# Delta-rule attention and two expert layers: the last three row tiles become two, one of them 288 rows wide

## The chip, the cores and the metric

The kernel runs on one core of one Trainium2 chip. The metric is the device time of one execution in microseconds (us). Three timed runs of the kernel before took 984.87, 984.94 and 985.98 us; the median is 984.94. One further execution was profiled: its span, from the first to the last instruction, is 974.3 us.

## The reference

Three layers follow each other. First attention with a delta rule: for each of 4 x 8 heads a 48 x 48 state runs over 768 tokens.

```python
for t in range(S):
    kt, vt, bt = (k_n[:, :, t], v[:, :, t], beta[:, :, t, None])
    y[:, :, t] = np.einsum('bhd,bhde->bhe', q[:, :, t], state)
    v_old = np.einsum('bhde,bhd->bhe', state, kt)
    state = state + bt[:, :, :, None] * np.einsum('bhd,bhe->bhde', kt, vt - v_old)
```

The result is laid out as 3072 rows of 384. Each row then goes to one of 8 experts, by the largest of 8 logits, and is weighted by its softmax share.

```python
logits = x @ w_gate + modality_bias[modality_id]
e_idx = np.argmax(logits, axis=1)
...
    h = np.maximum(x[mask] @ w1[e], 0.0)          # 384 -> 1024
    out[mask] = gate_w[mask, None] * (h @ w2[e])  # 1024 -> 384
```

The third layer, here called the second expert, is the same for all rows: the largest of three products with 384 x 768 weights, then a product with 768 x 384.

```python
h = np.maximum(np.maximum(x @ w1, x @ w2), x @ w3)
return (h @ w_out).astype(np.float32)
```

## The kernel before, in words

Attention is done in 12 chunks of 64 tokens (C = 0 to 11). After each chunk its 256 rows are routed (route, L696): VectorE finds each row's expert and place, and POOL scatters the rows into xs, a table in DRAM with RS rows for each expert. Rows are then taken from xs in row tiles: a tile is up to 256 rows of one expert. select (L744) picks an expert on VectorE, in some ten operations on one partition, and writes the expert's number and the first row into ssel, which has one buffer; SP reads it into registers (L791, L792) and issues the tile's loads. A selection after chunks 1 to 10 wants an expert with a full 256 rows; the final ones take the expert with the most rows left. After the last chunk 256 zero rows are copied behind each expert's last row (pad_zero, L780: eight DMAs), so that a tile that is not full reads zero rows. Those have a row number past the end, and their output is dropped.

So there are 13 tiles: one after each of the chunks 1 to 11, then one more of 256 rows and one of 128. If rows are left after that, a loop on the device (L973) takes further tiles of 256; its count comes from remaining (L764).

Numbers are kept as two 16-bit parts, so each product is three matmuls. For a tile of w rows, tiles (L900) makes eight steps f:

- up (L819): the product hp of 128 hidden columns with the tile's rows mxT, 9 matmuls of w columns; ScalarE and VectorE split it into hh and hl.
- down (L835): 9 matmuls of w columns from hh and hl into accA (two products) and accB (one), which stand in PSUM over all eight steps.
- behind (L894): in steps 0 to 5 the tile before gets a step of the second expert (second, L856), 27 matmuls of its own width into pa (two products) and pb; ScalarE copies the first product to mt, VectorE takes the maximum with the other two, ScalarE and POOL split it into H. In steps 6 and 7 comes outp (L878): 18 matmuls of 384 columns for each 128 rows, scaled by ScalarE, scattered to the output by POOL.

After step 7, mid (L849) turns accA and accB into x2T, which the second expert reads. Weights come per step into ws (L802) through SP's DMA queue, with two buffers, and are split by ScalarE (wh) and POOL (wl).

The last tile's second expert runs alone, with nothing beside it (L925). PSUM has eight banks: two for accA and accB (psA), three in a ring (psM, tag m) which hp, pa, pb and po share, and three for attention (psC, psZ).

The order on each engine is made in two ways. The first part of the program is played as a list of steps in program order; from the bar in STEPS on, a scheduler orders the instructions of each engine by priorities, with a model of the engines. What side() wraps is placed ahead. The order is fixed when the program is built.

Of the kernel before, what the change touches and what calls it, by code (L numbers as in the profile page):

```python
# [7 lines left out]
F32 = mybir.dt.float32  # L8
# [11 lines left out]
RS = 3072 + 256  # L20
ZROW = 8 * RS
XROWS = ZROW + 256
XW = 784
# [94 lines left out]
class Kern:  # L118
# [29 lines left out]
    # ---------------------------------------------------------------- setup  # L148
    def setup(self):
# [24 lines left out]
        # room that the second expert's weights take later  # L174
# [7 lines left out]
    def zeros(self, eng, what, x, i=0):  # L182
        """A zeroed tile: only its diagonal blocks are written later."""
# [152 lines left out]
    # ---------------------------------------------------------------- keys and queries of a group  # L336
# [97 lines left out]
    # ---------------------------------------------------------------- key products and 32-token inverses  # L434
# [74 lines left out]
    # ---------------------------------------------------------------- preparation of a chunk  # L509
# [121 lines left out]
    # ---------------------------------------------------------------- chain  # L631
# [63 lines left out]
    # ---------------------------------------------------------------- routing  # L695
# [68 lines left out]
    def remaining(self):  # L764
# [5 lines left out]
        E.tensor_scalar(out=a, in0=a, scalar1=MAGIC, scalar2=MAGIC, op0=ALU.add, op1=ALU.subtract)  # L770
        r = mx.tile([1, 1], F32, name="sthr")
# [16 lines left out]
    # ---------------------------------------------------------------- experts  # L788
    def tile_load(self, si, w=256):
        nc, mx = self.nc, self.tp["x"]  # L790
        e = nc.sync.value_load(si[0:1, 0:1], min_val=0, max_val=7)  # L791
        row = nc.sync.value_load(si[0:1, 1:2], min_val=0, max_val=ZROW)  # L792
        T = dict(e=e, w=w, ws={}, wb={})
        T["xT"] = mx.tile([128, 6, 256], F16, name="mxT", bufs=3)[:, :, 0:w]
        nc.sync.dma_start_transpose(out=T["xT"], in_=self.xs[bass.ds(row, w), 0:384].bitcast(F16))
        T["ix"] = mx.tile([128, 2, 2], I32, name="ix", bufs=3)
        nc.sync.dma_start(out=T["ix"][:, 0:w // 128], in_=self.xs[bass.ds(row, w), 384:386].rearrange("(t p) w -> p t w", p=128))
# [4 lines left out]
    def wt_load(self, T, f):  # L802
        nc, e = self.nc, T["e"]
        ws = self.tp["w"].tile([128, 2, 384], F32, name="ws")
# [5 lines left out]
    def wt_cast(self, T, f):  # L810
        ws = T["ws"].pop(f)
        wh = self.tp["w"].tile([128, 2, 384], F16, name="wh", bufs=2)
        wl = self.tp["w"].tile([128, 2, 384], BF16, name="wl", bufs=2)
        with self.side():
            self.nc.scalar.activation(wh, ws, AF.Copy)  # L815
            self.lo("p", wl, ws, wh)
        T["wb"][f] = wh, wl

    def up(self, T, f):  # L819
        nc, mx, xT, w = self.nc, self.tp["x"], T["xT"], T["w"]  # L820
        wh, wl = T["wb"][f]
        h = self.tp["psM"].tile([128, 256], F32, name="hp", tag="m")[:, 0:w]
# [5 lines left out]
        hh = mx.tile([128, 256], F16, name="hh", bufs=2)[:, 0:w]  # L828
        hl = mx.tile([128, 256], F16, name="hl", bufs=2)[:, 0:w]
# [4 lines left out]

    def down(self, T, f):  # L835
        nc, w = self.nc, T["w"]
        if f == 0:
            pa = self.tp["psA"].tile([128, 2, 256], F32, name="accA")[:, :, 0:w]
            pb = self.tp["psA"].tile([128, 1, 256], F32, name="accB")[:, :, 0:w]
            T["acc"] = pa, pb  # L840
        hh, hl = T["h"]
        wh, wl = T["wb"].pop(f)
        pa, pb = T["acc"]
        for d, ps in enumerate((pa[:, 0], pa[:, 1], pb[:, 0])):
            ds = slice(128 * d, 128 * d + 128)
            for i, (a, b) in enumerate(((wh, hh), (wl, hh), (wh, hl))):
                nc.tensor.matmul(ps, lhsT=a[:, 1, ds], rhs=b, start=(f == 0 and i == 0 and d != 1), stop=(f == 7 and i == 2 and d > 0))  # L847

    def mid(self, T):  # L849
        x2T = T["x2T"] = self.tp["x"].tile([128, 6, 256], F16, name="x2T", tag="mxT", bufs=3)[:, :, 0:T["w"]]  # L850
        for ps, k, n in zip(T.pop("acc"), (0, 2), (2, 1)):
# [4 lines left out]
    def second(self, T, f):  # L856
        nc, mx, x2T, w = self.nc, self.tp["x"], T["x2T"], T["w"]
        if f == 0:
            T["H"] = {x: mx.tile([128, 6, 256], F16, name="H" + x, tag="H" + x) for x in "hl"}
# [10 lines left out]
        mt = mx.tile([128, 256], F32, name="mt", tag="ob", bufs=2)[:, 0:w]  # L870
        with self.side():
# [3 lines left out]
            nc.scalar.activation(T["H"]["h"][:, f, 0:w], mt, AF.Copy)  # L875
            self.lo("p", T["H"]["l"][:, f, 0:w], mt, T["H"]["h"][:, f, 0:w])

    def outp(self, T, t):  # L878
        nc, H = self.nc, T["H"]
        ts = slice(128 * t, 128 * t + 128)  # L880
        po = self.tp["psM"].tile([128, 384], F32, name="po", tag="m")
# [132 lines left out]
```

## Time and profile before

| | us |
|---|---|
| timed runs, median of 3 | 984.94 (984.87 to 985.98) |
| profiled execution, span | 974.3 |
| between the span and the median | 10.6 |
| eleventh tile's eight steps | 39.41 |
| twelfth tile's eight steps | 39.40 |
| thirteenth tile's eight steps (128 rows) | 33.39 |
| its second expert alone | 13.09 |
| from TensorE's last matmul to the end | 9.06 |

The page gives the profiled execution no total beside its span; 10.6 us is what lies between the span and the median of the timed runs. A window row gives a stretch, its length, and for each engine the busy time and the number of instructions; PEclk is the granted share of TensorE's full clock, 1.00 or 0.50. In a timeline a row's first number is the start, the second the duration; a matmul's duration overlaps the next one's, so the pitch is read from starts. What stands in brackets is the idle time of the engine just ahead and what ended it.

### The profile page before, as it was taken

The numbers are of one execution on the slowest core, as the hardware profiler recorded it, in microseconds if no ns is written. First come the engines' busy times: TensorE is split into PE (matmuls) and PEld (weight loads), VectorE is DVE, ScalarE is ACT, GpSimd is POOL, SyncE is SP. The second block draws the span as 40 slices with busy tenths as digits, with TensorE's granted clock in tenths as the row PEclk, the third lists the DMA queues.
The fourth block names the chain that finished last, engine by engine and source line by source line (L and its number), as shares of the span: only waits on it lengthen the run. The fifth ranks groups of instructions, "written<-read, shape, count | busy, mean of one in ns | idle before, by whom it ended". The sixth has DMA issues, their size and how long they took to land. (4 is left out here: it accounts for less than half of the span.)

```text
span 974.3 us, 25386 instructions
## 1 busy us (share of the span) xinstructions
PE 715.9 (73%) x9748; PEld 597.9 (61%) x9748; DVE 651.2 (67%) x1581; ACT 446.1 (46%) x894; POOL 553.7 (57%) x708
## 2 busy tenths in 40 slices
PE   1314610686359877678779877999899989999995
PEld 0213510575238666466568666788787868888885
DVE  7798897778896599859998589656464442222221
ACT  3436532674356453444446433364554534434432
POOL 7264366646767777446776478555546444444461
PEclk9999855697669999788899999999999999999998
DMA  7786688776796747665777743555532354423320
GB/s 114 175 167 166 107 216 207 186 146 159 195 222 133 179 115 176 135 140 131 161 170 192 147 110 92 125 144 99 141 85 91 106 192 122 115 82 107 97 68 19
DMA packets 360349, 134.76 MB, mean 138 GB/s; under 512 B 291225, under 2 KB 351655, under 8 KB 360096
## 3 DMA queue, kind: packets, MB, share of 16 engines
q1 hardware_dynamic: 357088, 123.56, 55.3%
q0 software_dynamic: 3136, 9.54, 2.7%
q8 instruction: 78, 1.28, 0.6%
q14 instruction: 47, 0.39, 0.1%
HBM read 80.45 MB, written 33.79 MB: 117 GB/s over the span
## 5 line engine op out<-in xcount | busy, mean ns | idle before, releaser
L138 POOL TENSOR_TENSOR wl<-ws,wh 128x768 bf16<-128x768 f32 x104 | 172.2, 1656 | 75.9 <-ACT wh L815 73.7
L868 PE MATMUL pa<-x2T,mwh 128*128 128x256 f16 (+1 forms) x936 | 170.6, 277 | 17.4 <-DVE x2T L140 10.2
L868 PEld LDWEIGHTS <-mwh 128*128 128x128 f16 x1404 | 137.4, 100 | 29.0 <-issue 11.7
L826 PE MATMUL hp<-mxT,wh 128*128 128x256 f16 (+1 forms) x624 | 125.0, 278 | 40.2 <-ACT wh L815 36.0
L868 PE MATMUL pa<-x2T,mwl 128*128 128x256 f16 (+1 forms) x468 | 128.0, 277 | 0.0
L138 POOL TENSOR_TENSOR Hl<-mt,Hh 128x256 f16<-128x256 f32 (+1 forms) x78 | 52.0, 666 | 116.1 <-ACT Hh L875 114.0
L815 ACT ACTIVATE wh<-ws 128x768 f16<-128x768 f32 x104 | 87.4, 840 | 38.8 <-PE accB L847 20.1
L832 DVE SCALAR_TENSOR_TENSOR hl<-hp,hh 128x256 f16<-128x256 f32 (+1 forms) x104 | 42.5, 409 | 77.7 <-ACT hh L831 77.0
L826 PEld LDWEIGHTS <-wh 128*128 128x128 f16 x624 | 62.0, 101 | 46.3 <-ACT wh L815 37.2
L868 PE MATMUL pb<-x2T,mwh 128*128 128x256 f16 (+1 forms) x468 | 89.6, 270 | 1.0 <-DVE mt L873 1.0
L144 PEld LDWEIGHTS <-bkh 128*128 128x128 f16 x560 | 55.2, 105 | 55.8 <-DVE bkh L432 23.9
L826 PE MATMUL hp<-mxT,wl 128*128 128x256 f16 (+1 forms) x312 | 86.1, 279 | 2.8 <-POOL wl L138 2.8
L502 DVE TENSOR_TENSOR stmp<-At,W 128x31 f32<-128x31 f32 (+29 forms) x155 | 83.2, 537 | 3.3 <-POOL At L491 0.3
L138 POOL TENSOR_TENSOR pl<-Pm,ph 64x512 f16<-64x512 f32 x48 | 56.9, 1185 | 50.2 <-ACT ph L628 41.3
L868 PEld LDWEIGHTS <-mwl 128*128 128x128 bf16 x702 | 69.9, 100 | 18.6 <-issue 10.2
L875 ACT ACTIVATE Hh<-mt 128x256 f16<-128x256 f32 (+1 forms) x78 | 31.7, 407 | 95.7 <-DVE mt L874 95.5
L847 PEld LDWEIGHTS <-wh 128*128 128x128 f16 x624 | 61.9, 101 | 20.0 <-issue 11.0
L504 DVE TENSOR_TENSOR W<-W,stmp 128x31 f32<-128x31 f32 (+29 forms) x155 | 71.3, 460 | 3.0
L873 DVE TENSOR_TENSOR mt<-pa,mt 128x256 f32<-128x256 f32 (+1 forms) x78 | 32.1, 411 | 59.7 <-ACT mt L872 55.1
L847 PE MATMUL accA<-hh,wh 128*128 128x256 f16 (+1 forms) x208 | 57.6, 277 | 9.5 <-ACT hh L831 9.2
L868 PE MATMUL pb<-x2T,mwl 128*128 128x256 f16 (+1 forms) x234 | 62.7, 270 | 0.0
L847 PE MATMUL accA<-hl,wh 128*128 128x256 f16 (+1 forms) x208 | 57.6, 279 | 5.5 <-DVE hl L832 5.3
(277 smaller groups left out, 2590.5 us busy)
## 6 DMA issues: line engine op xcount, KB each, us to landing
ws<-in_moe_w_dram SPq DMA_DIRECT2D x208, 192.0 KB
nd<-in_moe_w_dram SPq DMA_DIRECT2D x18, 384.0 KB
vf<-in_v_dram SPq DMA_DIRECT2D x48, 96.0 KB
ring<-in_k_dram SPq DMA_DIRECT2D x10, 384.0 KB
ring<-in_q_dram SPq DMA_DIRECT2D x10, 384.0 KB
xs<-xs SPq DMA_DIRECT2D x8, 392.0 KB
N<-Wd SPq DMA_DIRECT2D x48, 64.0 KB
Qdh<-tmh SPq DMA_DIRECT2D x6, 512.0 KB
```

The costliest lines, as they stand in the source:

```text
L138: nc.gpsimd.tensor_tensor(out=out, in0=in_, in1=hi, op=ALU.subtract)
L144: mm(out, lhsT=ah, rhs=bh, start=start, stop=False)
L502: E.tensor_tensor(out=tv, in0=At[:, j:j + 1, j + 1:].to_broadcast([128, m, n]), in1=W[:, r0:r1, j:j + 1].to_broadcast([128, m, n]), op=ALU ...
L504: E.tensor_tensor(out=W[:, r0:r1, j + 1:], in0=W[:, r0:r1, j + 1:], in1=tv, op=ALU.subtract)
L815: self.nc.scalar.activation(wh, ws, AF.Copy)
L826: nc.tensor.matmul(h, lhsT=a[:, 0, kk * 128:(kk + 1) * 128], rhs=xT[:, b], start=(n == 0), stop=(n == 8))
L832: nc.vector.scalar_tensor_tensor(out=hl, in0=h, scalar=0.0, in1=hh, op0=ALU.max, op1=ALU.subtract)
L847: nc.tensor.matmul(ps, lhsT=a[:, 1, ds], rhs=b, start=(f == 0 and i == 0 and d != 1), stop=(f == 7 and i == 2 and d > 0))
L868: nc.tensor.matmul(ps[i], lhsT=self.mw[a][:, i, kk, fs], rhs=x2T[:, b], start=(n == 0), stop=(n == 8))
L873: nc.vector.tensor_tensor(out=mt, in0=ps[1], in1=mt, op=ALU.max)
L875: nc.scalar.activation(T["H"]["h"][:, f, 0:w], mt, AF.Copy)
```

## The change

The tiles after chunks 1 to 10 stay. The selection after the last chunk and the two final ones become two final selections: the first for a tile of up to 288 rows, the second for one of 256. Attention's pools are closed ahead of them, and the wide tile gets pools of its own in the room that becomes free: its x tiles (mxw) and three accumulators of one bank each (psAw: accA, accC, accB). In the ring psM its second expert takes three buffers for each step, pa, pc and pb, one for each product, where a tile of 256 takes two. Each expert's room in xs, the zero rows and the pad copies grow from 256 to 288 rows; the zero rows are written by three DMAs. The wide tile's output has three pieces, of 128, 128 and 32 rows; the second and the third both come in step 7. Functions that had fixed widths take them from the tile.

```diff
-RS = 3072 + 256
+WIDE = 288
+RS = 3072 + WIDE
 ZROW = 8 * RS
-XROWS = ZROW + 256
+XROWS = ZROW + WIDE
...
+    def wide_pools(self, ctx):
+
+        return dict(self.tp, psA=self.pool(ctx, "psAw", 1, space=PSUM), x=self.pool(ctx, "mxw", 1), W=WIDE)
...
     def zero_rows(self):
-        self.nc.sync.dma_start(out=self.xs[ZROW:XROWS, :].rearrange("(r p) d -> p r d", p=128), in_=self.zero.to_broadcast([128, 2, XW // 2]))
+        for r, n in ((ZROW, 128), (ZROW + 128, 128), (ZROW + 256, WIDE - 256)):
+            self.nc.sync.dma_start(out=self.xs[r:r + n, :], in_=self.zero[0:n, 0])
...
         E.tensor_scalar(out=a, in0=a, scalar1=MAGIC, scalar2=MAGIC, op0=ALU.add, op1=ALU.subtract)
+        E.tensor_scalar_max(out=a, in0=a, scalar1=0.0)
...
     def pad_rows(self, r):
-        self.nc.sync.dma_start(out=self.xs[bass.ds(r, 256), :], in_=self.xs[ZROW:XROWS, :])
+        self.nc.sync.dma_start(out=self.xs[bass.ds(r, WIDE), :], in_=self.xs[ZROW:XROWS, :])
...
-        T["xT"] = mx.tile([128, 6, 256], F16, name="mxT", bufs=3)[:, :, 0:w]
+        T = dict(e=e, w=w, tp=tp, ws={}, wb={}, cols=[(t, min(128, w - t)) for t in range(0, w, 128)])
+        T["xT"] = mx.tile([128, 6, w], F16, name="mxT", bufs=3)
...
+        if w > 128 * full:
+            nc.sync.dma_start(out=T["ix"][0:w - 128 * full, full], in_=self.xs[bass.ds(row + 128 * full, w - 128 * full), 384:386])
...
+    def triple(self, pool, w, names, tag=None):
+
+        if w > 256:
+            ts = [pool.tile([128, w], F32, name=n, **(dict(tag=tag) if tag else {})) for n in names]
+            return ts, [(k, 1, t) for k, t in enumerate(ts)]
+        a = pool.tile([128, 2, w], F32, name=names[0], **(dict(tag=tag) if tag else {}))
+        b = pool.tile([128, w], F32, name=names[2], **(dict(tag=tag) if tag else {}))
+        return [a[:, 0], a[:, 1], b], [(0, 2, a), (2, 1, b)]
...
         if f == 0:
-            pa = self.tp["psA"].tile([128, 2, 256], F32, name="accA")[:, :, 0:w]
-            pb = self.tp["psA"].tile([128, 1, 256], F32, name="accB")[:, :, 0:w]
-            T["acc"] = pa, pb
+            T["acc"], T["out"] = self.triple(T["tp"]["psA"], w, ("accA", "accC", "accB"))
...
-        pa = self.tp["psM"].tile([128, 2, 256], F32, name="pa", tag="m")
-        pb = self.tp["psM"].tile([128, 256], F32, name="pb", tag="m")
-        ps = [pa[:, 0, 0:w], pa[:, 1, 0:w], pb[:, 0:w]]
+        ps, _ = self.triple(T["tp"]["psM"], w, ("pa", "pc", "pb"), "m")
...
         if f < 6:
             self.second(T, f)
-        elif f - 6 < T["w"] // 128:
-            self.outp(T, f - 6)
+        for t in range(len(T["cols"])):
+            if f == min(6 + t, 7):
+                self.outp(T, t)
...
-        if C >= 1:
-            self.sis.append((self.select(C == self.NC - 1),))
+        if 1 <= C < self.NC - 1:
+            self.sis.append((self.select(False),))
...
         self.play(then)
+        self.actx.close()
+        self.sis.append((self.select(True, WIDE), self.wide_pools(self.ctx)))
         self.sis.append((self.select(True),))
-        self.sis.append((self.select(True, 128), 128))
         for _ in self.moe:
             pass
-        self.actx.close()
         ri = self.remaining()
```

On VectorE after the last chunk, the first place shows the end of the selections, with the tile counter srem, and mid of the ninth tile (x2T). Before:

```order
L760 TENSOR_TENSOR ssel<-sred,zc 1x2
L770 TENSOR_SCALAR skey<-skey 1x8
L758 TENSOR_REDUCE sred<-sprod 1x2
L772 TENSOR_REDUCE sthr<-skey 1x1
L774 CAST srem<-sthr 1x1
L832 SCALAR_TENSOR_TENSOR hl<-hp,hh 128x256
L140 SCALAR_TENSOR_TENSOR x2T<-accA,x2T 128x512
L760 TENSOR_TENSOR ssel<-sred,zc 1x2
L140 SCALAR_TENSOR_TENSOR x2T<-accB,x2T 128x256
```

On VectorE at the same place after the change:

```order
L777 TENSOR_SCALAR skey<-skey 1x8
L779 TENSOR_REDUCE sthr<-skey 1x1
L781 CAST srem<-sthr 1x1
L844 SCALAR_TENSOR_TENSOR hl<-hp,hh 128x256
L766 TENSOR_TENSOR ssel<-sred,zc 1x2
L844 SCALAR_TENSOR_TENSOR hl<-hp,hh 128x256
L141 SCALAR_TENSOR_TENSOR x2T<-accA,x2T 128x512
L141 SCALAR_TENSOR_TENSOR x2T<-accB,x2T 128x256
```

Of the two writes of ssel shown before one is gone, and the other stands ahead of both pieces of x2T.

On SP after the pad copies, the second place shows the register loads (ssel, srem) and the eleventh tile's transposing load. Before:

```order
L791 TENSOR_LOAD ssel
L791 ISA x2
L792 TENSOR_LOAD ssel
L792 ISA x2
L972 TENSOR_LOAD srem
L972 ISA x2
L791 TENSOR_LOAD ssel
L791 ISA x2
L792 TENSOR_LOAD ssel
L792 ISA x2
L795 ISA
L795 DMA_TRANSPOSE mxT<-xs 128x6x256
```

On SP at the same place after the change:

```order
L800 TENSOR_LOAD ssel
L800 ISA x2
L801 TENSOR_LOAD ssel
L801 ISA x2
L993 TENSOR_LOAD srem
L993 ISA x2
L804 ISA
L804 DMA_TRANSPOSE mxT<-xs 128x6x288
```

One selection's register loads are gone; the load stands at the same place, 32 columns wider.

On VectorE in the closing stretch, the third place shows mid of the second tile from the end and the first step behind it (hl is the last tile's, mt the second expert's). Before:

```order
L140 SCALAR_TENSOR_TENSOR x2T<-accA,x2T 128x512
L140 SCALAR_TENSOR_TENSOR x2T<-accB,x2T 128x256
L832 SCALAR_TENSOR_TENSOR hl<-hp,hh 128x128
L873 TENSOR_TENSOR mt<-pa,mt 128x256
L874 TENSOR_TENSOR mt<-pb,mt 128x256
```

On VectorE at the same place after the change:

```order
L141 SCALAR_TENSOR_TENSOR x2T<-accA,x2T 128x288
L141 SCALAR_TENSOR_TENSOR x2T<-accC,x2T 128x288
L141 SCALAR_TENSOR_TENSOR x2T<-accB,x2T 128x288
L844 SCALAR_TENSOR_TENSOR hl<-hp,hh 128x256
L893 TENSOR_TENSOR mt<-pc,mt 128x288
L894 TENSOR_TENSOR mt<-pb,mt 128x288
```

The twelfth tile of 256 rows stood there with the 128-row tile behind it; now the wide tile stands there with the 256-row tile behind it, and each product has a buffer of its own.

## Rows read from the trace of the kernel before

**Rows 1.** the page: busy us (share of the span) xinstructions; then one costly group

```profile
PE 715.9 (73%) x9748; PEld 597.9 (61%) x9748; DVE 651.2 (67%) x1581; ACT 446.1 (46%) x894; POOL 553.7 (57%) x708
...
L815 ACT ACTIVATE wh<-ws 128x768 f16<-128x768 f32 x104 | 87.4, 840 | 38.8 <-PE accB L847 20.1
```

**Rows 2.** windows of closing stages: stretch, length; busy (x) per engine; PEclk, DMA

```profile
839.91:879.32 39.41, 39.41 (x345) 33.45 (x343) 9.52 (x22) 16.20 (x32) 19.07 (x16) 1.00 0.35 101
879.32:918.72 39.40, 39.40 (x343) 33.46 (x342) 9.52 (x22) 16.20 (x32) 19.06 (x16) 1.00 0.33 97
918.72:952.11 33.39, 33.13 (x353) 28.41 (x351) 8.46 (x22) 13.80 (x32) 17.43 (x15) 1.00 0.27 84
952.11:965.20 13.09, 12.41 (x180) 10.78 (x179) 4.05 (x14) 4.13 (x15) 3.53 (x7) 1.00 0.04 14
965.20:974.26 9.06, 0.00 (x0) 0.00 (x0) 0.00 (x0) 0.58 (x1) 0.99 (x1) 0.70 0.03 9
```

**Rows 3.** timeline of TensorE: start us, us, engine, line, operation, names, shape

```profile
845.96 0.27 PE L826 MATMUL hp<-mxT,wh 128*128 128x256 f16 x1
...
850.87 0.27 PE L826 MATMUL hp<-mxT,wh 128*128 128x256 f16 x1
...
957.59 0.22 PE L868 MATMUL pa<-x2T,mwh 128*128 128x128 f16 x1
...
962.11 0.33 PE L885 MATMUL po<-moh,Hh 128*128 128x384 f16 x1
...
964.87 0.33 PE L885 MATMUL po<-moh,Hl 128*128 128x384 f16 x1
```

**Rows 4.** timeline of TensorE around 800: in brackets idle time and releaser

```profile
801.04 0.38 PE L868 MATMUL pa<-x2T,mwh 128*128 128x256 f16 x2 [2.96 <-DVE x2T L140]
...
806.30 0.28 PE L826 MATMUL hp<-mxT,wh 128*128 128x256 f16 x1 [1.77 <-ACT wh L815]
```

**Rows 5.** timeline of VectorE around 800

```profile
800.50 0.15 DVE L760 TENSOR_TENSOR ssel<-sred,zc 1x2 int32<-1x2 f32 x1 [4.16 <-SPq L792]
800.58 0.41 DVE L140 SCALAR_TENSOR_TENSOR x2T<-accB,x2T 128x256 f16<-128x256 f32 x1
```

**Rows 6.** timeline of ScalarE around 800

```profile
805.41 0.84 ACT L815 ACTIVATE wh<-ws 128x768 f16<-128x768 f32 x1 [2.11 <-DMA ws<-in_moe_w_dram]
```

**Rows 7.** timeline of SP's DMA queue around 800

```profile
790.42 5.70 SPq L778 DMA_DIRECT2D xs<-xs  x8
...
796.39 0.39 SPq L805 DMA_DIRECT2D ws<-in_moe_w_dram  x1
...
803.24 2.27 SPq L795 DMA_TRANSPOSE mxT<-xs  x1
```

**Rows 8.** windows while the pads move, columns as in rows 2

```profile
795.00:800.00 5.00, 3.08 (x27) 2.46 (x26) 0.69 (x1) 1.25 (x3) 1.00 (x1) 1.00 1.00 372
```

**Rows 9.** windows around two pauses of TensorE, columns as in rows 2

```profile
606.85:611.06 4.21, 0.00 (x1) 0.01 (x1) 4.08 (x11) 0.00 (x0) 1.91 (x2) 0.93 0.01 2
...
611.06:613.80 2.74, 2.74 (x55) 2.40 (x56) 2.63 (x10) 1.07 (x3) 0.81 (x2) 0.50 0.01 3
...
477.33:484.15 6.82, 5.86 (x41) 3.12 (x42) 6.68 (x13) 2.61 (x7) 4.88 (x7) 0.50 1.12 247
```

**Rows 10.** timeline of SP's DMA queue in the setup

```profile
39.79 0.85 SPq L298 DMA_DIRECT2D xs<-zero  x1
```

**Rows 11.** timeline of TensorE in the setup

```profile
71.33 0.21 PE L145 MATMUL Pp<-stl,bkh 128*128 128x64 f16 x1 [1.60 <-DMA stl<-tml]
```

**Rows 12.** timeline of TensorE after the last tile's products

```profile
952.61 0.22 PE L868 MATMUL pa<-x2T,mwh 128*128 128x128 f16 x1 [0.50 <-ACT x2T L853]
```

**Rows 13.** tile x2T: duration ns min/median/max, first and last start, forms

```profile
L140 DVE SCALAR_TENSOR_TENSOR x2T<-accA,x2T x13: 424/681/693, 249.3 to 952.6; 128x512 f16<-128x512 f32 x12, 128x256 f16<-128x256 f32 x1
```

**Rows 14.** timeline of ScalarE in a steady step

```profile
858.99 0.38 ACT L872 ACTIVATE mt<-pa 128x256 f32<-128x256 f32 x1 [1.58 <-PE pa L868]
```

**Rows 15.** timeline of VectorE in the same step

```profile
859.41 0.42 DVE L873 TENSOR_TENSOR mt<-pa,mt 128x256 f32<-128x256 f32 x1 [1.54 <-ACT mt L872]
```

More of the change, by code (lines that the diff above doesn't have):

```diff
@@ L837, in down @@
         if f == 0:
-            pa = self.tp["psA"].tile([128, 2, 256], F32, name="accA")[:, :, 0:w]
-            pb = self.tp["psA"].tile([128, 1, 256], F32, name="accB")[:, :, 0:w]
-            T["acc"] = pa, pb
+            T["acc"], T["out"] = self.triple(T["tp"]["psA"], w, ("accA", "accC", "accB"))
         hh, hl = T["h"]
         wh, wl = T["wb"].pop(f)
-        pa, pb = T["acc"]
-        for d, ps in enumerate((pa[:, 0], pa[:, 1], pb[:, 0])):
+        first = (0, 2) if w <= 256 else (0, 1, 2)
+        last = (1, 2) if w <= 256 else (0, 1, 2)
+        for d, ps in enumerate(T["acc"]):
             ds = slice(128 * d, 128 * d + 128)
             for i, (a, b) in enumerate(((wh, hh), (wl, hh), (wh, hl))):
-                nc.tensor.matmul(ps, lhsT=a[:, 1, ds], rhs=b, start=(f == 0 and i == 0 and d != 1), stop=(f == 7 and i == 2 and d > 0))
+                nc.tensor.matmul(ps, lhsT=a[:, 1, ds], rhs=b, start=(f == 0 and i == 0 and d in first), stop=(f == 7 and i == 2 and d in last))
     def mid(self, T):
-        x2T = T["x2T"] = self.tp["x"].tile([128, 6, 256], F16, name="x2T", tag="mxT", bufs=3)[:, :, 0:T["w"]]
-        for ps, k, n in zip(T.pop("acc"), (0, 2), (2, 1)):
+        w = T["w"]
+        x2T = T["x2T"] = T["tp"]["x"].tile([128, 6, w], F16, name="x2T", tag="mxT", bufs=3)
+        for k, n, ps in T.pop("out"):
+            ps = ps if n > 1 else ps[:, None]
             with self.side():
@@ L856, in second @@
     def second(self, T, f):
-        nc, mx, x2T, w = self.nc, self.tp["x"], T["x2T"], T["w"]
+        nc, mx, x2T, w = self.nc, T["tp"]["x"], T["x2T"], T["w"]
         if f == 0:
-            T["H"] = {x: mx.tile([128, 6, 256], F16, name="H" + x, tag="H" + x) for x in "hl"}
+            T["H"] = {x: mx.tile([128, 6, w], F16, name="H" + x, tag="H" + x) for x in "hl"}
         fs = slice(128 * f, 128 * f + 128)
-        pa = self.tp["psM"].tile([128, 2, 256], F32, name="pa", tag="m")
-        pb = self.tp["psM"].tile([128, 256], F32, name="pb", tag="m")
-        ps = [pa[:, 0, 0:w], pa[:, 1, 0:w], pb[:, 0:w]]
+        ps, _ = self.triple(T["tp"]["psM"], w, ("pa", "pc", "pb"), "m")
         for i in range(3):
@@ L884, in outp @@
             for a, b in (("h", "h"), ("h", "l"), ("l", "h")):
-                nc.tensor.matmul(po, lhsT=H[a][:, f, ts], rhs=self.mo[b][:, f], start=(i == 0), stop=(i == 17))
+                nc.tensor.matmul(po[0:n], lhsT=H[a][:, f, at:at + n], rhs=self.mo[b][:, f], start=(i == 0), stop=(i == 17))
                 i += 1
-        ob = self.tp["x"].tile([128, 384], F32, name="ob", bufs=2)
+        ob = T["tp"]["x"].tile([128, 384], F32, name="ob", bufs=2)
         with self.side():
-            nc.scalar.activation(ob, po, AF.Copy, scale=T["ix"].bitcast(F32)[:, t, 1:2])
+            nc.scalar.activation(ob[0:n], po[0:n], AF.Copy, scale=T["ix"].bitcast(F32)[0:n, t, 1:2])
         nc.gpsimd.indirect_dma_start(
-            out=self.out[:, :], out_offset=bass.IndirectOffsetOnAxis(ap=T["ix"][:, t, 0:1], axis=0), in_=ob, in_offset=None,
+            out=self.out[:, :], out_offset=bass.IndirectOffsetOnAxis(ap=T["ix"][0:n, t, 0:1], axis=0), in_=ob[0:n], in_offset=None,
             bounds_check=self.NT * 128 - 1, oob_is_err=False)
```

40 lines of the change are left out of this document (21 added, 19 removed).

## The prediction

> **What bounds the kernel now.** I read the page first. TensorE is busy for 73% of the span [rows 1], which does not say that it bounds anything, so I went to the windows over the last stretch, one for each row tile, cut where TensorE starts a tile's first matmul. From 839.91 to 918.72 the two 256-row tiles, the eleventh and the twelfth, take 39.41 and 39.40 us, with TensorE busy for all of it at the full granted clock (1.00, 2.4 GHz) and no other engine over 19.1 us [rows 2]. This stretch is TensorE's alone: what its matmuls take is what the stretch takes. Then come 33.39 us for the 128-row tile beside the twelfth's second expert, 13.09 us for the second expert of the 128-row tile alone, and 9.06 us in which TensorE does nothing [rows 2]: the last scatter and the end of the program, which the change leaves alone. Next I read TensorE's timeline for the pitch from start to start. From 845.96 to 850.87 there are 45 matmuls of 256 columns: 0.1091 us each. From 957.59 to 962.11 there are 81 of 128 columns: 0.0558. From 962.11 to 964.87 there are 17 steps of 384 columns: 0.1624 [rows 3]. So time follows the columns, down to 128.
>
> **The change: the matmuls.** A tile of at most 256 rows needs 8x9 matmuls for the up product, 8x9 for the down product and 6x27 for the second expert, 306 in all, each as wide as the tile; and 18 of 384 columns for each piece of up to 128 rows. Before, the last three tiles are 256, 256 and 128 wide; after, 288 and 256. So 306 matmuls of 256 and 306 of 128 columns go, and 306 of 288 come. The 384-column ones stay: 2+2+1 pieces before, 3+2 after, 90 either way, since the piece of 32 rows streams the same 384 columns. No row has 288 columns. Its bounds are the rows on both sides, 0.1091 and 0.1624. I take the line between them, 0.1091 + 32 x (0.1624 - 0.1091)/128 = 0.1224. Removed: 306 x (0.1091 + 0.0558) = 50.5. Added: 306 x 0.1224 = 37.5. **Gain 13.0 us.** At 0.1091 it would be 17.1, at 0.1624 only 0.8; both are far, since the three pitches lie on one line to within 0.001.
>
> The three rows lie on one line of columns [rows 3]. The Trainium skill, in its page "TensorE: Matmul & The Clock Gate", section "Back-to-back issue gap", says that in a real stream of weight loads and matmuls the pitch is about 81 ns at 128 columns and 131 ns at 512. On a straight line between these 256 and 288 columns would take 98 and 102 ns, an estimate from that page, and the gain would be 306 x (0.098 + 0.081 - 0.102) = 23.6 us. The rows contradict it at both widths (55.8 and 109.1 ns), and the sum goes by them.
>
> **The start of the tenth tile.** Ahead of the closing stretch stands one disturbed place. TensorE waits 2.96 us until 801.04 for VectorE's x2T, and 1.77 us until 806.30 for ScalarE's wh [rows 4]. VectorE is late there because it stands 4.16 us at the third ssel, which has one buffer and waits until SP has read the second; the last x2T is queued behind it [rows 5]. With one selection fewer that wait goes: in the new order the last ssel stands ahead of both x2T, and SP has read the one before it long ago. But what is late next is the weights. ScalarE's wh at 805.41 waited 2.11 us for the DMA of ws [rows 6], issued at 796.39, behind the eight pad copies of 5.70 us [rows 7]. So TensorE gets through its old work about 4 us sooner and then stands at the same matmul: this wait is worth nothing.
>
> The pads grow from 256 to 288 rows: 8 x 32 x 1568 bytes = 0.40 MB more ahead of ws. DMA moves 372 GB/s there, fully busy (share 1.00) [rows 8]: +1.1 us (0, if the ws packets slip between, to 2.2, if the copy costs a read and a write). Then TensorE idles from about 800 to 807 at a stretch. After a pause of 4.21 us it ran the next 2.74 us at 0.50 (1.2 GHz); the longest such stretch with dense work I found is 6.82 us [rows 9]. Half of each is lost: 1.4 us, at most 3.4, at least 0. Before, the half-rate work lay ahead of the wait for wh and cost nothing. I take +1.4.
>
> **The rest.** Setup writes the zero rows with three DMAs instead of one. One takes 0.85 us of SP's queue [rows 10], which issues without a pause there, and TensorE at 71.33 waits for a transpose from the same queue [rows 11]: three issues of 0.85 and two steps between make up to +1.9, and 0 if they are short; about half of a delay of 0.8 should survive 700 us of other waits: +0.4. When the last tile's products are done, TensorE waits 0.50 us for x2T [rows 12]; VectorE's first piece of it is now twice as wide and takes 0.68 us, where the 128-row tile's took 0.42 [rows 13]: +0.3 (0 to 0.5, if ScalarE's copy ahead of it grows as much). The wide tile's transpose, its extra index load on SP and the buffers taken from the attention cost nothing: attention's last scatter is out before the pads, and the load is issued near 803 [rows 7] for use at 840, 35 us of cover; were that gone, it would stall TensorE by what it is late. The matmuls of the tenth tile are put in another order, with the same count. The 32-row scatter runs behind the second scatter on POOL, while TensorE has 17 us of the last second expert ahead.
>
> **Sum.** -13.0 + 1.1 + 1.4 + 0.4 + 0.3 = -9.8 us. The profiled execution has a span of 974.3 us; the three timed runs have a median of 984.94, so 10.6 us lie around the span, which I leave as they are. Span 964.5, **time 975.1 us**.
>
> **Rivals.** First, PSUM. The wide tile's second expert needs three buffers per step (pa, pc, pb) beside hp, and the ring has three, where pa used to hold two products in one. Each product now takes the place of the one emptied three products ago. If emptying were exposed in each of six steps: 0.38 + 3 x 0.42 (ScalarE's mt [rows 14], VectorE's two maxima and hl, alike [rows 15]) = 1.64 us, six times 9.8, time 984.9, no change. Against it: between a product's end and the matmul that takes its place stand at least nine matmuls of another, 1.1 us for an emptying of 0.4 to 0.8. The Trainium skill, in "Perfetto Trace Analysis", section "Optimization Strategy", warns that the same gap repeating on the engine that should be saturated can mean too little PSUM for the next tile. The stretch of before shows no such gap [rows 2]; by that sentence the wide phase would be 9.8 us longer.
>
> Second, nothing is given back at the start of the tenth tile (weights land as before, clock stays up): 984.9 - 13.0 + 0.7 = 972.7.
>
> Third, on the other side: two tiles do not hold what is left, and the loop at the end, which did not run before (104 wh casts are 13 tiles of 8 [rows 1]), runs once. Ten full tiles leave 512 rows. The reference's own routing gives 1508 and 1564 tokens to two experts, so 228 and 284 remain, and 288 and 256 hold them, with 4 rows to spare on the wide one. It decides from 289 on. The price is a tile with nothing beside it: at least 39.4 us [rows 2] and its load, say 5: 1020.
>
> Fourth, the pitch leaves the line in the other direction: the weight loads beside the matmuls set it, and 288 columns cost no more than 256. Then the gain is 17.1, and the time 984.9 - 17.1 + 3.2 = 971.0. Against it: 384 columns cost their share in full [rows 3]. The Trainium skill's figures in "TensorE: Matmul & The Clock Gate", cited above, would go further the same way, to 984.9 - 23.6 + 3.2 = 964.5.
>
> **How the numbers follow.** Forecast with its own range of 973 to 980: 0.75. Nothing given back: 0.11. PSUM: 0.05. The loop: 0.04. The pitch off the line: 0.02. Something unseen: 0.03, spread evenly. With all costs at their lower ends the time is 971.9, at their upper ends (2.2, 3.4, 1.9, 0.5) 979.9; I widen by 0.6 to 0.9 on both sides, 971.0 to 980.8, which leaves out the loop and PSUM. What a measurement tells from no change is 0.2%, 2 us. Faster: 0.75 + 0.11 + 0.02 and 0.04 from the milder ends of PSUM and the unseen, 0.92; within 0.2%: 0.03; slower: 0.05.
>
> **What would show it.** In the profile after: no fourteenth tile; no VectorE wait at ssel; TensorE idle until about 807 for wh, with a ws landing about 1 us later and a half-rate stretch behind it; 288-column matmuls at a pitch of 0.122; the wide tile's phases of about 41.2 and 44.4 us without gaps; then 17.7 us of second expert and 5.8 us of output. The forecast is wrong if the pitch at 288 is off the line, if a gap stands in each wide step, or if TensorE starts the tenth tile before 806.

## The result and the profile after

| | before | after |
|---|---|---|
| first timed runs, median of 4, us | 984.9 (983.59 to 985.98) | 975.96 (971.72 to 976.4) |
| ratio, 95% interval | | 0.9907 (0.9882 to 0.9932) |
| timed again, us | 983.11, 29 runs | 975.16, 6 runs |
| ratio, 95% interval | | 0.9918 (0.9895 to 0.9942) |
| span of the profiled execution | 974.3 | 974.7 |

A ratio is to the kernel before, timed along with the kernel in question, and an execution that lasted far longer than its kernel's others is left out of it (experiment 8 has one of 1787.88 us, the one that was profiled). The forecast was 975.1 us, in a range of 971.0 to 980.8. The kernel became faster by 8 to 9 us. But the two profiled executions have nearly the same span, where the forecast had 964.5 for after. This contradiction had to be settled first (experiment 1): it was the profiled execution of before that lay at the quick end of its kernel's scatter.

The page of the profile after, the lines that answer to [rows 1]:

```profile
PE 701.5 (72%) x9442; PEld 580.6 (60%) x9442; DVE 646.8 (66%) x1552; ACT 434.8 (45%) x865; POOL 538.7 (55%) x694
...
L827 ACT ACTIVATE wh<-ws 128x768 f16<-128x768 f32 x96 | 80.5, 839 | 42.3 <-PE accB L867 21.5
```

96 wh casts are 12 tiles of 8: one tile fewer, and the loop at the end did not run.

Windows of after: the tenth tile's steps, a pause inside them and the stretch behind it, the wide tile's steps, the last tile's steps beside the wide tile's second expert, the last second expert with its output, and the end. Columns as in [rows 2].

```profile
801.27:850.66 49.39, 42.33 (x345) 34.78 (x342) 9.24 (x22) 16.16 (x32) 19.10 (x16) 0.90 0.49 151
807.49:814.54 7.05, 0.00 (x0) 0.00 (x1) 0.53 (x2) 1.26 (x2) 1.16 (x2) 0.68 0.90 261
814.54:820.20 5.66, 5.66 (x27) 4.04 (x28) 0.42 (x1) 1.23 (x2) 3.23 (x2) 0.50 0.70 173
850.66:891.88 41.22, 41.22 (x343) 33.48 (x342) 9.79 (x22) 16.59 (x32) 19.06 (x16) 1.00 0.33 97
891.88:938.06 46.18, 45.82 (x371) 35.94 (x369) 10.10 (x24) 16.72 (x36) 18.95 (x17) 1.00 0.21 65
938.06:961.83 23.77, 23.77 (x198) 19.27 (x197) 6.10 (x14) 5.49 (x14) 4.74 (x7) 1.00 0.01 4
961.83:974.69 12.86, 0.00 (x0) 0.00 (x0) 0.00 (x0) 0.58 (x1) 1.98 (x2) 0.70 0.09 30
```

From the eleventh tile's first matmul to TensorE's last it is 961.83 - 850.66 = 111.17 us; before it was 965.20 - 839.91 = 125.29 [rows 2]. So 14.1 us went there. But the tenth tile takes 49.39 us, and the end takes 12.86 where [rows 2] has 9.06.

TensorE in the wide tile's second expert; nine matmuls of pa and nine of pc start between the two rows, which gives 2.21 / 18 = 0.1228 us:

```profile
899.24 0.29 PE L888 MATMUL pa<-x2T,mwh 128*128 128x288 f16 x1
...
901.45 0.27 PE L867 MATMUL accA<-hh,wh 128*128 128x256 f16 x1
```

The start of the tenth tile's products, on TensorE, ScalarE, SP and VectorE in turn; these answer to [rows 4 to 7]:

```profile
814.54 0.40 PE L838 MATMUL hp<-mxT,wh 128*128 128x256 f16 x1 [7.06 <-ACT wh L827]
```

```profile
813.64 0.84 ACT L827 ACTIVATE wh<-ws 128x768 f16<-128x768 f32 x1 [5.07 <-DMA ws<-in_moe_w_dram]
```

```profile
797.56 5.74 SPq L785 DMA_DIRECT2D xs<-xs  x8
803.57 0.39 SPq L817 DMA_DIRECT2D ws<-in_moe_w_dram  x1
```

```profile
795.34 0.65 DVE L766 TENSOR_TENSOR ssel<-sred,zc 1x2 int32<-1x2 f32 x1 [0.66 <-SPq L801]
```

VectorE waits 0.66 us at the last ssel where it stood 4.16. TensorE now stands once, for 7.06 us, until 814.54. From the first pad's issue to the wh that TensorE needs it is 813.64 - 797.56 = 16.08 us; before it was 805.41 - 790.42 = 14.99 [rows 6, 7]. That is the 1.1 us of the bigger pads; over more traces it is 1.3 (below).

The last scatters on POOL:

```profile
961.97 1.01 POOL L910 DMA_INDIRECT out_dram<-ob,ix  x1 [4.31 <-ACT ob L909]
966.50 0.97 POOL L910 DMA_INDIRECT out_dram<-ob,ix  x1 [3.52 <-DMA out_dram<-ob,ix]
```

The second scatter waits 3.52 us, and what ends the wait is the landing of the first. The last tile of before had one piece and so one scatter behind TensorE's last matmul, 0.95 us behind it:

```profile
966.15 0.99 POOL L890 DMA_INDIRECT out_dram<-ob,ix  x1 [2.44 <-ACTq L973]
```

From the last scatter's start to the end it is 8.1 us before and 8.2 after, so the wait of the second scatter is the difference. This wait was not in the forecast.

### The profile page after: what moved, and what is told of

It reads as the page before. It is cut to its first block, busy times and chain, and to the rows that moved or that the text cites. A ratio compares the mean times of both kernels' runs of the same rounds, so it can differ in the third digit from the quotient of the medians.

```text
span 974.7 us, 24604 instructions
## 1 busy us (share of the span) xinstructions
PE 701.5 (72%) x9442; PEld 580.6 (60%) x9442; DVE 646.8 (66%) x1552; ACT 434.8 (45%) x865; POOL 538.7 (55%) x694
## 4 chain that ended last, share of the span: by engine, by line
PE 29%; DVE 28%; DMA 7%; issue 6%; POOL 4%; ACT 3%; SPq 3%; POOLq 0%; DVEq 0%; ACTq 0%
PE pa L888 7%; DVE stmp L508 6%; PE hp L838 5%; DVE W L510 4%; PE pb L888 4%; PE po L905 4%; PE accA L867 3%; DMA xT<-xt 2%; PE accB L867 1%; DMA ws<-in_moe_w_dram 1%; DVE tl L581 1%; DMA xs<-xt,slot 1%; SPq L474 1%; POOL wl L139 1%; DVE hl L844 1%
## 5 line engine op out<-in xcount | busy, mean ns | idle before, releaser
L139 POOL TENSOR_TENSOR wl<-ws,wh 128x768 bf16<-128x768 f32 x96 | 159.2, 1659 | 71.3 <-ACT wh L827 69.4
L888 PE MATMUL pa<-x2T,mwh 128*128 128x256 f16 (+1 forms) x828 | 159.7, 284 | 14.7 <-DVE x2T L141 6.9
L838 PE MATMUL hp<-mxT,wh 128*128 128x256 f16 (+1 forms) x576 | 119.4, 283 | 49.1 <-ACT wh L827 42.3
L888 PEld LDWEIGHTS <-mwh 128*128 128x128 f16 x1296 | 129.8, 101 | 27.1 <-issue 7.6
L888 PE MATMUL pa<-x2T,mwl 128*128 128x256 f16 (+1 forms) x414 | 117.5, 284 | 0.0
L827 ACT ACTIVATE wh<-ws 128x768 f16<-128x768 f32 x96 | 80.5, 839 | 42.3 <-PE accB L867 21.5
L838 PEld LDWEIGHTS <-wh 128*128 128x128 f16 x576 | 57.7, 101 | 53.8 <-ACT wh L827 44.8
L867 PEld LDWEIGHTS <-wh 128*128 128x128 f16 x576 | 57.6, 101 | 24.7 <-issue 15.6
L893 DVE TENSOR_TENSOR mt<-pa,mt 128x256 f32<-128x256 f32 x66 | 27.8, 421 | 61.1 <-ACT mt L892 57.5
L147 PEld LDWEIGHTS <-bkl 128*128 128x128 f16 x560 | 55.0, 106 | 8.3 <-issue 4.5
L867 PE MATMUL accA<-hh,wh 128*128 128x256 f16 (+1 forms) x184 | 52.0, 282 | 10.0 <-ACT hh L843 10.0
```

The lines of the kernel that those rows point to most:

```text
L139: nc.gpsimd.tensor_tensor(out=out, in0=in_, in1=hi, op=ALU.subtract)
L147: mm(out, lhsT=al, rhs=bh, start=False, stop=stop)
L838: nc.tensor.matmul(h, lhsT=a[:, 0, kk * 128:(kk + 1) * 128], rhs=xT[:, b], start=(n == 0), stop=(n == 8))
L888: nc.tensor.matmul(ps[i], lhsT=self.mw[a][:, i, kk, fs], rhs=x2T[:, b], start=(n == 0), stop=(n == 8))
```

## Experiments

### 1. The kernel before, unchanged, twice

No edit. The first of them, e1:

> The kernel before, unchanged, to see how its span and its time hang together. Before's profiled execution had a span of 974.3 us where its timed runs had a median of 984.94; the changed kernel's profiled execution had a span of 974.7 us and a time of 976.38, 1.7 us apart. Theory A: what lies around the span is 1.7 us for any kernel, and before's profiled execution was some 9 us quicker than its timed runs, so new executions show spans of 982 to 984 us, with the extra time spread over the attention stretch ahead of 794 us, and the closing stretch from the eleventh tile on unchanged at 125.3 us to TensorE's last matmul. Theory B: before has 10 us around its span, so new spans are near 974 with times of 985.

Measured: 12 timed runs, median 980.64 us (977.16 to 986.42), each 1.7 us above its own span. The profiled one took 977.16 us with a span of 975.4. So theory A holds in the 1.7 us and B falls. Theory A's spans of 982 to 984 us were too narrow: the twelve spans lie between 975.4 and 984.6, and two of them are in that range. Later a third profile, e12:

> A third profile of the kernel before. Two profiled executions took 976.0 (974.3 of span and 1.7 around it) and 977.2 us, where its timed runs lie between 975.6 and 986.4 with a median near 982. If chance chose the two, this one is anywhere in that range, and its tenth tile begins later than 793.8 to 794.9 by what it is longer, with the same stages from there on. If a profiled execution of this kernel is quicker by itself, it is again 976 to 977.

Measured: 982.74 us, span 981.0. Its windows, from the tenth tile to the end:

```profile
798.49:846.59 48.10, 44.02 (x344) 35.30 (x342) 9.39 (x23) 16.22 (x32) 19.01 (x16) 0.89 0.49 153
846.59:886.00 39.41, 39.41 (x344) 33.46 (x342) 9.52 (x22) 16.22 (x32) 19.09 (x16) 1.00 0.35 101
886.00:925.41 39.41, 39.41 (x345) 33.45 (x342) 9.52 (x22) 16.22 (x32) 19.10 (x16) 1.00 0.33 97
925.41:958.80 33.39, 33.12 (x352) 28.40 (x351) 8.46 (x22) 13.81 (x32) 17.47 (x15) 1.00 0.26 84
958.80:971.89 13.09, 12.41 (x180) 10.78 (x179) 4.05 (x14) 4.13 (x15) 3.54 (x7) 1.00 0.04 14
971.89:980.96 9.07, 0.00 (x1) 0.00 (x0) 0.00 (x0) 0.58 (x1) 0.99 (x1) 0.71 0.03 9
```

The closing stretch repeats to 0.01 us (125.30 to TensorE's last matmul). What differs between executions of one and the same kernel lies ahead of it: the ninth tile's steps end at 793.84, 794.93 and 798.49, and the tenth tile's own stretch is 46.07, 46.09 and 48.10 us. The execution that the prediction was read from was the quickest of the three.

### 2. The kernel after, unchanged

> The changed kernel, unchanged, for the ratio with a narrower interval and a second trace. By the forecast's terms: about 0.990 of before (975 to 976 us). TensorE's pause ahead of the tenth tile's first products again near 7 us, behind it a half-rate stretch, the wide tile's own phase 41.2 us. If the 7.4 us by which the first trace of this kernel reaches the tenth tile later than the first trace of before is chance, a second trace is off by another amount, up or down by several us; if it is the change (three zero-row DMAs, other code), it is again 6 to 8 us behind the 793.84 of the first trace of before, and also behind a new trace of before.

Measured: ratio 0.9918 (0.9895 to 0.9942). The second trace has the pause at 7.28 us, the tenth tile's stretch at 49.41, the wide tile's at 41.23 and the end at 12.65 us. It reaches the tenth tile at 801.88 and the first trace of after at 801.27, 7.4 us behind the first trace of before. That alone looked like a cost of the change. But the traces of the variants below spread as widely. The six with the tiles of before (its three, e3, e4, e11) get there at 793.84 to 798.85, on the mean 796.4; the seven with the wide tile (both of after, e5 to e8, e10) at 796.37 to 802.27, on the mean 799.8. So the 7.4 us are mostly scatter, and 3.3 us are left between the means. The timed runs do not show these 3.3 us. An estimate takes from their medians 1.7 us and the mean stretches of the traces from the tenth tile on (46.75 + 125.30 + 9.07 and 49.40 + 111.17 + 12.75): before then reaches the tenth tile at 983.11 - 1.7 - 181.1 = 800.3 us, after at 975.16 - 1.7 - 173.3 = 800.2. Of the 3.3 us, 0.9 may be the VectorE instruction of the last section, 2.8 us shorter in two of the six; where the rest comes from is not shown.

### 3. The pads alone, on the kernel before

```diff
-RS = 3072 + 256
+WIDE = 288
+RS = 3072 + WIDE
...
-        self.nc.sync.dma_start(out=self.xs[bass.ds(r, 256), :], in_=self.xs[ZROW:XROWS, :])
+        self.nc.sync.dma_start(out=self.xs[bass.ds(r, WIDE), :], in_=self.xs[ZROW:XROWS, :])
```

with the three zero-row DMAs of the change.

> The kernel before with only the rooms, the zero rows (three DMAs) and the pad copies of 288 rows; its tiles stay 256, 256 and 128. By the forecast's terms: setup +0.4 us, pads +1.1 us ahead of the ws that the tenth tile waits for, so 1.5 us slower in all (0 to 4), about 1.0015 of before; in the trace the ws behind the pads is issued later by about 0.5 us and TensorE's wait for the tenth tile's wh grows by about 1. Rival: the pads are not what delays ws, then no change at all in the wait for wh (1.8 us).

Measured: 984.86 us, ratio 1.0035 (1.0014 to 1.0057), so 1.4 to 5.6 us slower. The price of 1.5 is at the low end. The trace shows 16.27 us from the first pad's issue to wh; it is 14.99, 14.58 and 14.62 in the three traces of before. Its tenth tile's stretch:

```profile
797.02:846.82 49.80, 43.64 (x344) 35.30 (x342) 9.39 (x23) 16.16 (x32) 19.10 (x16) 0.90 0.47 148
```

That is 1.7 to 3.7 above theirs, though TensorE's wait for wh itself is only 2.10 us, where the three traces of before have 1.77, 0.52 and 0.81: the rest stands in the wait for x2T (4.06, where they have 2.96 to 3.21) and in the granted clock of 0.90. The eleventh tile's stretch is longer too, 40.28 us for 39.41. The rival falls: the pads delay ws.

### 4. Two buffers for ssel, on the kernel before

```diff
-        si = mx.tile([1, 2], I32, name="ssel")
+        si = mx.tile([1, 2], I32, name="ssel", bufs=2)
```

> The kernel before with two buffers for ssel, so that VectorE does not stand 4.16 us at the third selection. By the forecast this wait is worth nothing, because the ws behind the pads is next late: ratio 1.000 (0.999 to 1.001), the wait at x2T (2.96 us) gone and the wait for wh grown by as much, from 1.8 to near 5 us. Rival: the wait is on the path, and the kernel is 3 to 4 us faster (0.996 to 0.997).

Measured: ratio 0.9997 (0.9977 to 1.0018). TensorE's one pause there:

```profile
807.54 0.40 PE L826 MATMUL hp<-mxT,wh 128*128 128x256 f16 x1 [5.92 <-ACT wh L815]
```

The wait at x2T is gone, and 1.77 us of wait for wh have become 5.92, where the two waits of [rows 4] together were 4.73. The tenth tile's stretch is 48.12 us, as in the third trace of before. The forecast's claim holds: this wait is worth nothing as long as the pads hold back ws.

### 5. The last tile's output products in order

TensorE keeps the order as written: all six parts of the first piece, then those of the second, where the scheduler had put the last part of both behind the first five of both.

```diff
-        for f in range(8):
-            self.behind(prev, f)
+        for f in range(6):
+            self.behind(prev, f)
+        with self.tc.manual_schedule(engines={mybir.EngineType.PE}):
+            for f in range(6, 8):
+                self.behind(prev, f)
```

> The changed kernel with the two output products of the last tile in order: the first piece's 18 matmuls all before the second's. Theory (the tail grew because both scatters become ready together and the second waits for the first one's landing): the first scatter starts near 2.4 us earlier, its landing then lies beside the second product, TensorE's last matmul stays where it is and the stretch from there to the end falls from 12.8 us to 10 to 10.8; time 2 to 2.8 us below the changed kernel, near 0.9895 of before. Rival (the end waits for something that the order of the products does not set): the stretch stays near 12.8 us.

Measured: ratio 0.9879 (0.9852 to 0.9906). The end, as a window, and the two scatters:

```profile
955.94:965.53 9.59, 0.00 (x0) 0.00 (x0) 0.00 (x0) 0.58 (x1) 0.97 (x1) 0.73 0.07 24
```

```profile
953.97 1.00 POOL L910 DMA_INDIRECT out_dram<-ob,ix  x1 [2.20 <-ACT ob L909]
957.35 0.97 POOL L910 DMA_INDIRECT out_dram<-ob,ix  x1 [2.38 <-ACTq L997]
```

From TensorE's last matmul to the end it is 9.59 us where it was 12.86: 3.3 us less, a little more than forecast. The landing of the first scatter now lies beside the second product, and the matmuls lose nothing by the order: from the eleventh tile's first to the last it is 955.94 - 844.77 = 111.17 us, as in after. The ratio fell by 0.0039, 3.8 us, and the intervals are 3 us on either side, so it is the trace that shows the wait to be the cost of the end. Of the 3.7 us, 0.5 are left: the second scatter starts 1.41 us behind TensorE's last matmul, where that of before started 0.95 behind. What holds it there is not shown.

### 6. Pads behind the tenth tile's first weights

```diff
-        if C == self.NC - 1:
-            self.pad_zero()
...
+    def pads(self):
+        self.pad_zero()
...
-route1.11@1012 sub.5@1013
+route1.11@1012 pads@1040 sub.5@1013
```

> The changed kernel with the pad copies at a later place in the order, so that SP issues the tenth tile's first ws behind one pad copy instead of eight, and its second behind six. Theory (the pads ahead of ws keep TensorE waiting 7 us, and the idle time then costs 10.2 us of half rate): no pause over 2 us ahead of the tenth tile's first products, no half-rate stretch there, its phase 40 to 42 us instead of 49.4, time 7 to 9 us below the changed kernel, near 0.984 of before. Rival 1 (half rate is not due to the pause): phase 44 to 45, time 4 to 5 us lower. Rival 2 (ws lands late in any order, since the pads share the DMA engines): phase 47 to 49, time within 2 us of the changed kernel.

Measured: ratio 0.9851 (0.9827 to 0.9875). SP issues the first ws behind one pad copy and the second behind six:

```profile
795.49 0.67 SPq L785 DMA_DIRECT2D xs<-xs  x1
796.43 0.39 SPq L817 DMA_DIRECT2D ws<-in_moe_w_dram  x1
...
797.60 3.52 SPq L785 DMA_DIRECT2D xs<-xs  x5
801.37 0.39 SPq L817 DMA_DIRECT2D ws<-in_moe_w_dram  x1
```

The tenth tile's stretch:

```profile
798.03:840.79 42.76, 40.29 (x343) 33.20 (x342) 9.52 (x22) 16.09 (x32) 19.09 (x16) 1.00 0.56 178
```

The clock stays at 1.00 and the longest pause is 1.56 us, for ScalarE's hh. 49.39 - 42.76 = 6.6 us, and the ratio says the same (0.0067); 7 to 9 were expected, and the stretch is 0.8 above the range given. Both rivals fall: the pads share the DMA engines with ws here too, but what made ws late was its place in SP's queue.

### 7. A wide tile of 320 rows

```diff
-WIDE = 288
+WIDE = 320
```

> The changed kernel with the wide tile of 320 rows instead of 288 (rooms, zero rows and pads with it). On the line of the three pitches 320 columns take 0.1091 + 64 x 0.0533 / 128 = 0.1357 us: 144 + 162 matmuls by 0.0133 more are +1.9 us in the wide tile's own phase (41.2 to 43.1) and +2.2 in the next (its second expert); the pads are 0.40 MB more again, +1.1 by the forecast's price: 5.2 us above the changed kernel, 0.997 of before. If 32 more rows of pad cost what the pads alone did on the kernel before (3.4 us in the times), it is 7.5 above, 0.9995. If the pitch were set by the weight loads up to some width, the phases would stay at 41.2.

Measured: ratio 0.9955 (0.9932 to 0.9979), against 0.9918 for 288: 3.6 us slower, with an interval of 3 on either side. 5.2 or 7.5 us were expected; the first lies within the interval, the second does not. Windows of the tenth tile, the wide tile, and the rest to TensorE's last matmul:

```profile
799.00:848.94 49.94, 42.17 (x343) 34.69 (x342) 9.24 (x22) 16.15 (x32) 19.09 (x16) 0.90 0.50 157
848.94:891.93 42.99, 42.99 (x344) 33.46 (x342) 10.06 (x22) 16.77 (x32) 19.06 (x16) 1.00 0.32 93
891.93:964.17 72.24, 71.88 (x569) 55.42 (x566) 16.70 (x37) 22.28 (x49) 23.85 (x23) 1.00 0.14 43
```

The wide tile's stretch went from 41.22 to 42.99 (+1.77, expected 1.9), the rest from 46.18 + 23.77 = 69.95 to 72.24 (+2.29, expected 2.2). The line of columns holds above 256 too. The tenth tile's stretch grew by 0.5 us for the pads' next 32 rows, half of the 1.1 expected.

### 8. One DMA for the zero rows

```diff
-        for r, n in ((ZROW, 128), (ZROW + 128, 128), (ZROW + 256, WIDE - 256)):
-            self.nc.sync.dma_start(out=self.xs[r:r + n, :], in_=self.zero[0:n, 0])
+        self.nc.sync.dma_start(out=self.xs[ZROW:XROWS, :].rearrange("(r p) d -> p r d", p=96), in_=self.zero[0:96].to_broadcast([96, 3, XW // 2]))
```

> The changed kernel with the 288 zero rows written by one DMA (96 partitions, three rows each) instead of three. Theory (two more issues on SP delay the setup): SP's time for them falls from 1.75 to 2.04 us to 0.8 to 1.0, the first hp comes 1 to 1.4 us earlier (near 175), time 0.5 to 1.4 us below the changed kernel. Rival (other waits hide it): first hp and time unchanged within their scatter.

Measured: ratio 0.9927 (0.9901 to 0.9953), no difference from 0.9918. The setup of this kernel is not shown; the next pair settles it.

### 9. The edits together, with one and with three zero-row DMAs

The edits of experiments 5 and 6, with that of 8 (e10) and without it (e7).

> The changed kernel with all three edits: last tile's output products in order, pads at the later place, zero rows in one DMA. If their worths add (3.3 us for the tail and 6.6 for the tenth tile's phase, both as the traces showed, and 0 to 1.2 for the zero rows): 10 to 11 us below the changed kernel, ratio to before 0.980 to 0.982; TensorE's last matmul to the end 9.6 us, the tenth tile's phase 42.8. Rival (the edits take from the same slack): over 0.984.

> As the kernel with all three edits, but with the zero rows in three DMAs as the change has them. If these cost 1.2 us of the setup, 1.2 us above the former and the first hp about 1 us later (176 against 175); if other waits hide them, the same time. The two should differ by less than 0.2%, so the first hp and SP's time for the zero rows decide more than the times.

Measured: e10 965.62 us, ratio 0.9825 (0.9781 to 0.9870); e7 963.65 us, ratio 0.9807 (0.9771 to 0.9843). Windows of e7, the tenth tile and the end:

```profile
799.55:842.13 42.58, 40.03 (x345) 33.37 (x343) 9.52 (x22) 15.88 (x32) 19.10 (x16) 1.00 0.56 183
953.17:962.76 9.59, 0.00 (x0) 0.00 (x0) 0.00 (x0) 0.58 (x1) 0.97 (x1) 0.78 0.08 24
```

Both worths are there, and they add (0.980 to 0.982 was expected). The three DMAs take 1.80 us of SP's queue (e7; 1.67 to 2.05 in all traces that have three), the one 0.63 (e10), and the first hp comes at 177.25 and 176.14. By the ninth tile nothing is left of that: 799.55 and 802.27, the other way round. So the zero rows' issues are hidden, and the rival of experiment 8 holds as far as the scatter lets one see. These two are the fastest kernels of the study; which is the better of them is not told by the times.

### 10. The kernel before with late pads

The edits of experiments 4 and 6 on the kernel before.

> The kernel before (tiles of 256, 256 and 128) with the pads at the later place and two buffers for ssel. By the theory its tenth tile too loses what the pads cost it: its phase falls from 46.1 to 41 to 43 us, and the time is 3 to 5 us below before (0.995 to 0.997). Against the changed kernel with late pads (0.9851) the gain of the wide tile alone is then 10 us, which the closing stretch gives (14.1 us fewer to TensorE's last matmul, 3.8 more in the tail). Rival (the changed kernel's larger pads and longer pause are a cost of the change alone): before gains under 1 us.

Measured: 976.1 us, ratio 0.9937 (0.9908 to 0.9967).

```profile
798.85:840.35 41.50, 39.73 (x345) 33.45 (x343) 9.43 (x22) 16.09 (x32) 19.08 (x16) 1.00 0.52 169
```

The kernel before had been paying there as well: the two edits together take 4.6 to 6.6 us from the tenth tile's stretch (46.07 to 48.10). Experiment 4 shows that the second buffer alone gives nothing; late pads alone were not tried on the kernel before. The gain in time, 6 us, is above what was expected (3 to 5) within its interval. With the pads late in both, the stretch from the tenth tile to the end is 974.79 - 798.85 = 175.94 us here and 964.47 - 798.03 = 166.44 in e6: the wide tile is worth 9.5 us, where the change as made got 7.8 (below). The difference is mostly in the tenth tile's stretch: with late pads it is 1.3 us longer with the wide tile (42.76 against 41.50), with early pads 2.6.

## Why the prediction was right, and where it was not

Term by term, in us. Stretches of before are means of its three traces, those of after of its two:

| term | forecast | traces |
|---|---|---|
| matmuls and waits, eleventh tile to TensorE's last matmul | -13.0 + 0.3 | -14.1 |
| tenth tile's stretch (46.75 to 49.40) | 1.1 + 1.4 | +2.6 |
| zero rows, where the ninth tile ends | +0.4 | not told from 0 |
| from TensorE's last matmul to the end (9.07 to 12.75) | 0 | +3.7 |
| sum | -9.8 | -7.8 |

The two timed medians differ by -8.9 and -8.0 us. That the forecast time of 975.1 lies within 1 us of both medians of after is luck in part. By the traces the forecast gain was 2.0 us too large: 3.7 us at the end were put at nothing, against 1.4 of gain too little and a setup term of 0.4 that does not show. And the median that it was taken off, 984.94, lies 1.8 us above that of the 29 later runs.

**Right: the pitch.** 0.1228 us at 288 columns against 0.1224 forecast, and the stretches with 320 follow the same line. The wide tile's stretch is 41.22 (41.2 forecast). The fourth rival falls. So does the 102 ns, an estimate worked out from the Trainium skill's "TensorE: Matmul & The Clock Gate", section "Back-to-back issue gap": the trace has 122.8.

**Too small: the gain of the closing stretch.** It is 1.4 above the forecast. The wait for x2T at the last second expert, which was to grow, is 0.36 us in the trace of after against 0.50 [rows 12]. And by columns the last two stretches ahead of the end of [rows 2] come to 72 x 0.0558 + 72 x 0.0558 + (9 + 162) x 0.1091 + 36 x 0.1624 = 32.5 and 162 x 0.0558 + 18 x 0.1624 = 12.0 us (nine products of the tile before fall into the first). They took 33.39 and 13.09: 2.0 us stood beside the columns, and the sum took off columns alone. In after the same count gives 45.4 and 23.5 for 46.18 and 23.77, only 1.0 us. (The forecast had 44.4 for the first of these: nine products of the wide tile's last step, 1.1 us, fall into it by the way the stretches are cut.) Which waits beside the 0.50 of [rows 12] made up the 2.0 was not tried.

**Right: the ssel wait is worth nothing, and ws is next late.** TensorE starts the tenth tile's products late, for wh, as forecast, 814.54 - 801.27 = 13.3 us into the stretch, where the forecast's 807 is 13.2; experiment 4 shows the exchange by itself, and experiment 6 takes the pads' place away and with it pause and half rate.

**Right in sum, wrong in parts: half rate.** The pads' 1.1 is confirmed to 0.2 us: from the first pad's issue to wh it is 14.8 us on the mean of four traces with pads of 256 rows (before's three and e4, 14.58 to 14.99) and 16.1 of four with 288 (after's two, e3 and e5, 15.85 to 16.27). What is left of the tenth tile's +2.6 is 1.3, near the 1.4 priced, but both parts of that price were off. Behind its pause after runs 5.66 us at 0.50, of which half, 2.8 us, is lost, twice the price. And the cover I named for before (half-rate work ahead of the wait for wh costs nothing) holds in the first trace alone, where the granted clock is 1.00 behind the wait:

```profile
806.30:812.00 5.70, 5.70 (x53) 5.12 (x54) 1.28 (x3) 2.21 (x5) 4.53 (x4) 1.00 0.57 149
```

In the third it stays at 0.50 for 4.60 us behind the wait, with 22 matmuls where the next 4.64 us have 45:

```profile
810.76:815.36 4.60, 4.60 (x22) 3.21 (x23) 0.00 (x0) 1.38 (x3) 3.86 (x3) 0.50 0.55 143
815.36:820.00 4.64, 4.64 (x45) 4.14 (x44) 1.27 (x3) 0.91 (x3) 0.67 (x1) 1.00 0.27 86
```

That is 2.3 us lost, and the stretch of the third trace is 2.0 us longer than that of the first.

**Failed: "the last scatter and the end of the program, which the change leaves alone".** The last tile now has two pieces, their products end 0.8 us apart, and the second scatter waits for the landing of the first, so 3.7 of the 14.1 us are given back. The prediction followed the queues of SP and VectorE through the change, and not POOL's behind TensorE's last matmul.

**Failed: "10.6 us lie around the span".** It is 1.7 in every run that has both numbers. The forecast took the difference of two executions for a fixed cost. It did no harm, since the gain was taken off the median of the timed runs, but the forecast span (964.5) was wrong by 10, and the profiled execution was the quickest of three. That the first timed runs were 9 us longer than the profiled one (974.3 + 1.7 = 976.0) is scatter up to the tenth tile, as far as traces show; where the timed runs, which leave no trace, spend it stays open.

**The other rivals.** PSUM: no gap stands in the wide tile's second expert, 162 matmuls at 0.122 to 0.123. Nothing given back: 2.6 us were given back at the start of the tenth tile (the rival's sum gives 972.6 and not 972.7). The loop did not run.

## What to carry to other kernels

When the last unit of work gets more pieces, follow each piece's output to its landing: here the second scatter into the same table waited for the landing of the first, and finishing the first early cost the matmuls nothing. When a transfer that nobody waits for yet stands ahead of one that TensorE needs, move it behind: here that took 6.6 us off the stretch. And compare a profiled execution's own time with the timed runs before reading a difference of a few us between two traces: here the same kernel's traces differed by 6.7 us.

## What had not been expected of the hardware

One VectorE instruction on 128x32 numbers, at 9.03 us with the same instruction ahead of it, took 0.93 us in the first two traces of before and 3.74 in the third, and 3.73 in both of after and in e4. ScalarE's step behind it came at 9.99 us in those two and at 12.79 to 12.82 in the others, of every kernel, so the change is not its cause. The step comes early enough to matter: the first hp of the two quick traces starts at 171.44 and 172.92, that of the third at 174.33. So 2.8 of the 4.7 and 3.6 us by which the third trace reaches the tenth tile later may stand here; why the instruction is longer is not shown. In the third trace of before:

```profile
9.03 3.74 DVE L365 TENSOR_SCALAR s<-ss 128x32 f32<-128x32 f32 x1
```

After nearly the same pause for x2T (2.96, 3.20 and 3.21 us) the three traces of before have a mean granted clock of 0.96, 0.93 and 0.89 in the tenth tile's stretch; at levels of 1.00 and 0.50 that is 2 x 0.04 x 46.07 = 3.7, 6.5 and 10.6 us at half rate. So behind pauses of nearly the same length the time at half rate varied by about 7 us between executions of one kernel, and the stretches by 2.0 us.
